# Four GpSimd operations tied behind VectorE's activation operation, and the engine orders solved anew

## The chip, the cores and the metric

The kernel runs on one core of a Trainium2 chip. A core has five engines with a queue each: TensorE (PE: matmuls; PEld: its weight loads), VectorE (DVE), ScalarE (ACT), GpSimd (POOL) and SyncE (SP, which here only issues DMAs). Each engine takes its instructions in order, and instructions of different engines meet only at semaphores. The metric is the device time of one execution in microseconds; before the change it is 293.84 us, the median of 3 runs (292.66 to 293.95).

## The reference

Two layers follow each other, in float32, for 8 batches of 576 tokens and 8 heads of 64:

```python
q_s = softmax(q, axis=-1)                 # over the 64 of a head
k_s = softmax(k, axis=2)                  # over the 576 tokens
kv  = einsum('bhsd,bhde->...', k_s, v)    # 64x64 per batch and head
x   = (q_s @ kv) as [4608 tokens, 512]
h   = x @ w_in                            # 512 -> 2048
g   = where(h > 0, h, exp(min(h, 0)) - 1) # ELU
out = g @ w_out                           # 2048 -> 512
```

## The kernel before

**Units of attention.** Each batch is two units n (16 in all, two per batch). For a unit the kernel loads q, k and v (576 KB each), takes `exp` of q and k on ScalarE (lines 392, 396, 416), row sums of q and their reciprocals on VectorE (418, 420), multiplies q by them (430, mostly GpSimd; tile QS), copies v to bfloat16 (a cast at line 274; tile VB), transposes QS (by TensorE for units 0 to 3, line 454; by a DMA transpose `turn`, line 467, from unit 4, whose result is copied into qsT by `widen`, again line 274), multiplies k by v on TensorE (`kv_mm`, 504), scales that into MBLK (513, 517) and multiplies MBLK by qsT (`ao_mm`, 535; `ao_parts`, 547). The result is copied from PSUM into XT (`xt`, line 274). Units 2 and 3 use one qsT buffer in turn.

**Blocks of the second layer.** The 4608 tokens are nine blocks j of 512. For each there are eight hidden groups g of 256 rows: `hg_mm` (line 617, eight matmuls of 128x512) writes a pair of PSUM banks, and `hg` makes the ELU of it. There are two forms of that. Form "a": ScalarE takes `exp` (643) and `relu(1-e)` (645), and VectorE ends it with `scalar_tensor_tensor` on two halves (649). Form "d", used for every second group of blocks 0 and 1 alone: ScalarE takes `exp` (643), VectorE takes min and add in place on the SBUF tile ESB (`tensor_scalar`, 654: this is the "activation operation" of the change), then a `tensor_tensor` max against PSUM (656). A block's next `hg_mm` on the same bank pair waits for the end of that. Two pairs of banks alternate, and ESB has two buffers. Blocks 0 and 1 multiply by `w_out` plainly (`out_mm`, 670). From block 2 on a product with seven in place of eight partial multiplications is used (`pair`, `mms`, 803): it needs combinations of the weights (`combos`, 730; tiles TB and W) and of the activations (`add_sum`, 754; tiles SB and GR), and its partial results are added at line 812.

**What sets the order.** The program adds 1395 operations, numbered as they are added, each with what it reads and writes; from that come its dependencies. `ORDER` lists, for each engine, the numbers in the order in which the engine takes them. An operation that may run on two engines goes to the one whose list holds its number. `Sched.order` merges the five lists into one program with modelled durations; `emit` turns each dependency on another engine into a semaphore wait. The lists are fixed text: nothing is decided on the chip. Spare matmuls (line 889) fill TensorE's first microseconds.

The operations that the change and the prediction name, all in the profile's stretch from 15 to 110 us:

| number | what it is | engine before | engine after |
|---|---|---|---|
| 68, 69, 70, 73 | loads: q of unit 2, `w_out` parts 0 and 1, q of unit 3 (GpSimd's queue) | POOL | POOL, order 69, 68, 70, 73 |
| 77, 76 | loads of v and k of unit 3 | POOL, 77 first | POOL, 76 first |
| 114, 122, 124, 137, 140 | exp of q of unit 2; ELU of block 0, group 6 (exp, max); exp and row sum of q of unit 3 | ACT, DVE | the same engines |
| 138 | exp of k of unit 3 | ACT | ACT |
| 151 | `ao_mm` of unit 2, second part | PE | PE, one `out_mm` earlier |
| 154 | copy of unit 3's transposes into qsT (after 151 has read it) | DVE | ACT |
| 146, 152 | `xt` copies of unit 2 | DVE | ACT |
| 179, 185, 188 (and 182) | copies of block 0's output from PSUM | DVE (182 ACT) | ACT |
| 166, 173 | `xt` copies of unit 3 | ACT | ACT, behind the eight above |
| 192, 194 | `hg_mm` of block 1, group 1, first and second half | PE | PE |
| 249, 250, 195 | exp and relu of block 1, group 1; exp of group 0 | ACT | ACT |
| 196, 255, 268, 281 | `tensor_scalar` (654) of block 1, groups 0, 2, 4, 6 | DVE | DVE |
| 197, 256, 269, 282 | `tensor_tensor` max (656) of the same | DVE | DVE |
| 253, 266, 279 | `hg_mm` of block 1, groups 2, 4, 6 | PE | PE |
| 208, 234, 237 | casts of v of units 5, 6, 7 | POOL | POOL |
| 210 | `widen` of unit 4 | POOL | ACT |
| 227, 300 | QS of units 5 and 6 | POOL | POOL |
| 239 | `kv_mm` of units 6 and 7 | PE | PE |
| 390 | a weight combination of group 1 | POOL, after 237 | POOL, ahead of 237 |
| 305, 316 | `xt` copies of units 6 and 7, first parts | ACT | DVE |
| 369 | copy of a block-1 output | ACT | DVE |
| 419 | row sum of q of unit 9 | DVE | DVE, ahead of block 3's 405 and 406 |

Of the kernel before, what the change touches and what calls it, by code (L numbers as in the profile page):

```python
# [11 lines left out]
B, H, S, D = 8, 8, 576, 64  # L12
# [12 lines left out]
ISSUE = {"sp": 550, "act": 550, "gp": 740}  # L25
ORDER = {
# [23 lines left out]
    "act": (  # L50
# [11 lines left out]
    "dve": (  # L62
# [37 lines left out]
}  # L100


class Op:
    __slots__ = ("eng", "dur", "emit", "deps", "key", "idx", "start", "end",
                 "dma", "sem", "val", "clock", "nbytes", "side", "early", "alts")

    def __init__(self, eng, dur, emit, key, dma=None, nbytes=0):
        self.eng, self.dur, self.emit, self.key = eng, dur, emit, key
# [938 lines left out]
        for i in range(4):  # L1047
            one[i]()
            two[i]()


S_ = S
# [32 lines left out]
```

## Time and profile before

| | |
|---|---|
| median of 3 runs | 293.84 us (292.66 to 293.95) |
| the profiled execution | 294.51 us, of which 292.7 us are the span from first to last instruction |
| busy: PE, DVE, ACT, POOL | 280.9, 234.7, 207.3, 165.7 us |
| mean granted TensorE clock | 0.999 |

The page gives busy times, the span in 40 slices and the chain of work that ended last. A busy PE counts pipelined matmuls with modelled ends, so a stall of TensorE is read best from the starts of its matmuls. In a row of the timeline come the start, the duration, the engine, the line, the operation and its tiles, the number of instructions merged, and in brackets the idle time before it and what ended that.

### The profile page before, as it was taken

Reading aid. Unit: us, or ns where it says so; the run is one execution under the profiler, and the core shown is the slowest. Engines: PE = TensorE matmul, PEld = TensorE weight load, DVE = VectorE, ACT = ScalarE, POOL = GpSimd, SP = SyncE. Lnnn points to the kernel's source line nnn. Section 1 sums busy time; section 2 is a strip of 40 time slices with the busy share of each in tenths; the row PEclk is TensorE's granted clock in tenths of the full one; section 3 lists DMA queues with packets and bytes.
Section 4 is the critical chain, followed back from the end, with each engine's and each line's share of the span. In section 5 each row is a group of like instructions: output and inputs, shape, how many; then the busy total and the mean of one; then the engine's idle time right before and its main releaser. Section 6 shows DMA issues by size and latency. Waiting matters only on the chain.

```text
span 292.7 us, 5471 instructions
## 1 busy us (share of the span) xinstructions
PE 280.9 (96%) x2176; PEld 243.2 (83%) x2176; DVE 234.7 (80%) x434; ACT 207.3 (71%) x227; POOL 165.7 (57%) x162
## 2 busy tenths in 40 slices
PE   2899999989999999999999999999999999999995
PEld 0478787767888889998999899899999999989994
DVE  3648848898878989969998989689888767698793
ACT  4868716958979988976987869967765636665520
POOL 2892445642756569577538383669505571575930
PEclk9999999999999999999999999999999999999999
DMA  7999997879996485937762926451302003200315
GB/s 264 399 365 389 388 389 261 246 230 287 273 215 250 140 216 136 274 82 236 145 198 57 279 59 186 142 107 38 76 18 56 0 17 74 54 0 20 92 38 143
DMA packets 36475, 50.04 MB, mean 171 GB/s; under 512 B 16353, under 2 KB 18145, under 8 KB 36449
## 3 DMA queue, kind: packets, MB, share of 16 engines
q1 hardware_dynamic: 29680, 33.96, 41.9%
q0 software_dynamic: 6528, 15.47, 17.5%
q8 instruction: 17, 0.28, 0.4%
q10 hardware_dynamic: 240, 0.26, 0.3%
q14 instruction: 10, 0.07, 0.1%
HBM read 36.70 MB, written 9.44 MB: 158 GB/s over the span
## 4 chain that ended last, share of the span: by engine, by line
PE 83%; DMA 7%; DVE 3%; POOL 3%; ACT 1%; issue 0%; SPq 0%
PE PS L617 38%; PE PS L803 32%; PE PS L670 9%; DMA W<-in_moe_w_out_dram 5%; PE PS L535 2%; DMA KR<-in_k_dram 2%; POOL W L374 2%; PE PS L504 2%; DVE ESB L654 1%; DVE GR L656 1%; ACT ESB L643 1%; DVE GR L649 0%; POOL VB L274 0%; PE PS L454 0%; POOL QS L430 0%
## 5 line engine op out<-in xcount | busy, mean ns | idle before, releaser
L617 PE MATMUL PS<-XT,W 128*128 128x512 f32 x576 | 142.3, 393 | 1.4 <-DVE GR L656 1.4
L617 PEld LDWEIGHTS PS<-XT,W 128*128 128x128 f32 x576 | 104.9, 188 | 23.1 <-DVE GR L656 2.2
L649 DVE SCALAR_TENSOR_TENSOR GR<-PS,GE 128x512 fp32r<-128x512 f32 x112 | 76.7, 687 | 19.9 <-ACT GE L645 18.5
L643 ACT ACTIVATE GE<-PS 128x1024 f32<-128x1024 f32 x56 | 57.4, 1024 | 40.6 <-PE PS L617 33.0
L754 POOL TENSOR_TENSOR GR<-GR 128x256 fp32r<-128x256 f32 (+1 forms) x55 | 50.9, 946 | 28.4 <-PE PS L803 22.8
L645 ACT ACTIVATE GE<-GE 128x1024 f32<-128x1024 f32 x56 | 59.4, 1061 | 1.5
L803 PE MATMUL PS<-W,GR 128*128 128x256 f32 x336 | 53.7, 283 | 0.0
L803 PE MATMUL PS<-TB,GR 128*128 128x256 f32 x336 | 52.2, 283 | 0.0
L803 PEld LDWEIGHTS PS<-W,GR 128*128 128x128 f32 x336 | 47.1, 191 | 1.2
L803 PEld LDWEIGHTS PS<-TB,GR 128*128 128x128 f32 x336 | 46.5, 191 | 1.1
L430 POOL TENSOR_TENSOR QS<-QR,RZQ 128x1152 f16<-128x1152 f32 (+1 forms) x16 | 31.1, 1941 | 24.0 <-DVE RZQ L420 22.8
L812 DVE TENSOR_TENSOR OSB<-OSB,PS 128x256 f32<-128x256 f32 x84 | 34.4, 416 | 8.1 <-PE PS L803 6.8
L670 PE MATMUL PS<-W,GR 128*128 128x512 f32 x128 | 33.1, 397 | 0.2 <-DMA W<-in_moe_w_out_dram 0.2
L754 POOL TENSOR_TENSOR SB<-GR 128x256 fp32r<-128x256 f32 (+1 forms) x19 | 17.2, 909 | 25.7 <-DVE GR L649 15.3
L754 POOL TENSOR_TENSOR GR<-SB,GR 128x256 fp32r<-128x256 f32 (+1 forms) x18 | 18.5, 1034 | 16.9 <-PE PS L803 16.7
L670 PEld LDWEIGHTS PS<-W,GR 128*128 128x128 f32 x128 | 23.2, 188 | 5.3 <-DMA W<-in_moe_w_out_dram 0.7
L418 DVE TENSOR_REDUCE ZQ<-QR 128x18 f32<-128x1152 f32 (+2 forms) x18 | 21.7, 1208 | 6.4 <-ACT QR L416 5.1
L396 ACT ACTIVATE KR<-KR 128x1152 bf16<-128x1152 f32 x16 | 18.3, 1155 | 8.4 <-DMA KR<-in_k_dram 8.4
L643 ACT ACTIVATE ESB<-PS 128x1024 f32<-128x1024 f32 x16 | 16.1, 1024 | 6.9 <-PE PS L617 5.9
L754 DVE TENSOR_TENSOR GR<-GR 128x256 fp32r<-128x256 f32 (+1 forms) x29 | 19.5, 675 | 0.3
L274 POOL CAST VB<-VR 128x1152 bf16<-128x1152 f32 (+1 forms) x11 | 11.9, 1083 | 12.9 <-DMA VR<-in_v_dram 10.8
L803 PE MATMUL PS<-W,SB 128*128 128x256 f32 x104 | 17.6, 282 | 0.0
(62 smaller groups left out, 272.1 us busy)
## 6 DMA issues: line engine op xcount, KB each, us to landing
out_dram<-OSB SPq DMA_DIRECT2D x61, 128.0 KB, 2.5
QR<-in_q_dram SPq DMA_DIRECT2D x12, 576.0 KB, 4.6
KR<-in_k_dram SPq DMA_DIRECT2D x12, 576.0 KB, 4.8
VR<-in_v_dram SPq DMA_DIRECT2D x12, 576.0 KB, 5.4
W<-in_moe_w_out_dram POOLq DMA_DIRECT2D x4, 1024.0 KB, 17.0
QR<-in_q_dram POOLq DMA_DIRECT2D x4, 576.0 KB, 11.8
VR<-in_v_dram POOLq DMA_DIRECT2D x4, 576.0 KB, 13.3
KR<-in_k_dram POOLq DMA_DIRECT2D x4, 576.0 KB, 11.1
```

What stands on the lines that cost most here:

```text
L274: return e.activation(dst, src, AF.Copy) if e is self.nc.scalar else e.tensor_copy(dst, src)
L396: S.add("act", t_act(1152, False), lambda e: e.activation(ek[:, :, :, :].rearrange("p h c d -> p (h c d)"), flat(k), AF.Exp), key - 2, X=[ ...
L418: S.add("dve", t_dve(m), lambda e, qp=qp, zp=zp: e.tensor_reduce(zp, qp, AX.X, ALU.add), key - 3, R=[f"qR{i}{x}" for x in xs], W=[f"ZQ{i}{ ...
L430: lambda e, qp=q[:, :, a:b, :], rz=rz, dst=qs[:, :, a:b, :]: e.tensor_tensor(dst, qp, rz, ALU.mult),
L617: last = e.matmul(P[:, t * 512:(t + 1) * 512], self.W1[:, kc, tt * 128:(tt + 1) * 128], self.XT[:, kc, rc:rc + BLK], start=(kc == 0), stop ...
L643: S.add("act", t_act(1024, True), lambda e: e.activation(ge, P, AF.Exp), key, W=own, X=banks)
L645: S.add("act", t_act(1024, False), lambda e: e.activation(ge, ge, AF.Relu, bias=1.0, scale=-1.0), key, X=own)
L649: S.add("dve", t_dve(512 if j else 1024), lambda e, u=u: e.scalar_tensor_tensor(*(x[:, :, u, :] if j else x for x in (gt, P)), 0.0, ge[:, ...
L670: last = e.matmul(dst, self.tile(jb, jj, ts), self.W2[:, jj, c0:c1], start=(jj == 0), stop=(jj == 15))
L754: lambda e: e.tensor_tensor(dst, a, b, op), key, R=R, W=W, X=X, after=after)
L803: last = e.matmul(dst, a[i][:, y_, :], b[i][:, y_, :], start=start and i == 0 and y_ == 0, stop=stop and i == len(grps) - 1 and y_ == z - ...
L812: S.add("dve", t_dve(256), lambda e: e.tensor_tensor(dst, a, b, ALU.add), key, R=R, W=W, X=X, after=after)
```

## The change

Four dependencies are added at the end of the program, so that four GpSimd operations wait for VectorE's line 654 in block 1: the cast of v of unit 5 for group 0, QS of unit 5 for group 2, the cast of v of unit 6 for group 4, QS of unit 6 for group 6. All five lists of `ORDER` are replaced from about the seventieth operation on. 125 operations change their engine: 40 go from GpSimd to VectorE and 37 back, 24 from VectorE to ScalarE and 12 back, 7 from ScalarE to GpSimd and 5 back. No operation is added or removed, and TensorE's operations stay the same in number and size.

```diff
     "act": (
-        "3 29 25 41 22 36 23 45 53 34 38 39 58 66 67 90 93 94 96 100 101 104 111 112 114 122 134 "
-        "109 135 137 126 115 138 182 198 173 166 224 249 250 195 199 207 254 260 261 267 297 273 "
-        "274 221 280 230 236 286 287 233 293 294 308 334 240 335 343 344 407 352 353 305 317 358 "
+        "3 29 25 41 22 36 23 45 53 34 38 39 58 66 90 93 94 96 100 101 104 111 112 114 108 122 134 "
+        "109 137 135 126 115 146 154 152 138 179 182 198 185 188 173 166 224 249 250 195 207 199 "
+        "254 260 261 210 267 297 273 274 221 280 223 230 286 232 287 233 293 294 236 334 335 308 "
...
     "dve": (
-        "106 113 117 123 118 108 124 119 140 141 142 136 128 129 130 146 152 179 154 160 161 162 "
-        "185 174 167 201 188 202 225 251 252 196 197 255 256 212 262 213 226 214 263 215 216 217 "
-        "268 269 298 275 276 223 281 299 282 232 288 289 386 348 295 296 309 339 241 310 242 336 "
+        "105 106 113 117 123 118 124 119 140 141 136 142 128 129 130 160 161 162 174 167 201 202 "
+        "225 226 251 252 196 197 255 256 262 263 212 213 214 215 216 217 268 269 275 276 281 298 "
+        "282 299 288 289 348 295 296 240 241 242 243 336 337 244 245 309 246 310 345 305 346 354 "
...
     "gp": (
-        "1 32 14 15 24 16 17 18 48 40 19 20 21 68 69 70 73 72 71 74 75 77 76 120 131 116 143 163 "
-        "144 139 164 132 200 205 203 208 210 227 234 300 237 390 394 318 303 311 387 410 314 395 "
+        "1 32 14 15 24 16 17 18 48 40 19 20 21 69 68 70 73 72 71 74 75 76 77 120 131 116 143 163 "
+        "144 139 132 164 200 205 203 208 227 234 300 390 237 394 303 386 318 311 399 388 410 392 "
...
     "sp": (
-        "8 9 10 11 12 13 204 206 209 219 228 187 184 218 180 235 229 189 302 238 301 190 349 350 "
+        "8 9 10 11 12 13 204 206 183 180 187 189 186 209 228 190 218 219 235 229 301 302 184 238 "
...
+AFTER = ((208, 196), (227, 255), (234, 268), (300, 281))
...
             one[i]()
             two[i]()
+        for a, b in AFTER:
+            S.ops[a].deps.setdefault(S.ops[b], "raw")
```

In SP's list 204 and 228 are DMA transposes, 206, 209, 218, 219, 229 and 235 loads of units 6 and 7, and 180 to 190 the eight output stores of block 0 (128 KB each): five of the stores now stand ahead of 209, the load of v of unit 6.

119 rows, old and new, of the table ORDER are left out of this document.

## The prediction

> **What bounds the kernel now.** I read the page first (busy times, clock, the chain that ended last), then busy times by stretch, then what TensorE waited for, and then the timeline of the one stretch in which it waited.
>
> ```profile
> span 292.7 us, 5471 instructions
> PE 280.9 (96%) x2176; PEld 243.2 (83%) x2176; DVE 234.7 (80%) x434; ACT 207.3 (71%) x227; POOL 165.7 (57%) x162
> ...
> PEclk9999999999999999999999999999999999999999
> ...
> PE 83%; DMA 7%; DVE 3%; POOL 3%; ACT 1%; issue 0%; SPq 0%
> ```
>
> TensorE is busy for 96% of the span at full clock, and is 83% of the chain. The change leaves its work alone, so the time can move only by what TensorE waits. The next rows give, for three stretches, the busy time of PE, PEld, DVE, ACT and POOL in turn:
>
> ```profile
> 14.00:50.00 36.00, 35.78 (x274) 28.57 (x275) 25.14 (x38) 22.26 (x26) 18.58 (x23) 1.00 1.22 357
> 50.00:72.00 22.00, 20.55 (x158) 15.89 (x157) 19.53 (x29) 16.89 (x18) 10.45 (x8) 1.00 0.86 257
> 72.00:289.00 217.00, 217.00 (x1680) 195.56 (x1678) 182.53 (x349) 158.80 (x172) 129.55 (x119) 1.00 0.45 121
> ```
>
> From 72 to 289 us TensorE is never idle; from 14 to 50 it loses 0.2 us; the loss is in 50 to 72, which is block 1, where VectorE has 19.53 of 22 us. What TensorE waited for there, and line 654 over the whole run (minimum, median, maximum in ns):
>
> ```profile
> PE PS L617 <- DVE GR L656: 1.4, 2, 0.9
> ```
> ```profile
> L654 DVE TENSOR_SCALAR ESB<-ESB x8: 683/690/1612, 19.5 to 69.6; 128x1024 f32<-128x1024 f32 x8
> ```
>
> Two waits for line 656; and line 654 just ahead of it takes 0.69 us as a rule and 1.61 at worst. The timeline shows where:
>
> ```profile
> 56.11 1.15 POOL L274 CAST VB<-VR 128x1152 bf16<-128x1152 f32 x1 [2.23 <-DMA VR<-in_v_dram]
> 56.23 1.94 ACT L643 ACTIVATE ESB<-PS 128x1024 f32<-128x1024 f32 x2 [0.32 <-DVE GR L656]
> ...
> 57.20 1.15 POOL L274 CAST qsT<-QT 128x1152 fp32r<-128x1152 f16 x1
> 57.29 1.61 DVE L654 TENSOR_SCALAR ESB<-ESB 128x1024 f32<-128x1024 f32 x1 [1.09 <-ACT ESB L643]
> ...
> 58.54 0.73 PE L670 MATMUL PS<-W,GR 128*128 128x512 f32 x2
> ...
> 58.93 1.22 DVE L656 TENSOR_TENSOR GR<-ESB,PS 128x1024 fp32r<-128x1024 f32 x1
> ...
> 60.21 2.11 PE L617 MATMUL PS<-XT,W 128*128 128x512 f32 x8 [0.94 <-DVE GR L656]
> ...
> 63.33 1.15 POOL L274 CAST VB<-VR 128x1152 bf16<-128x1152 f32 x1
> 63.42 1.61 DVE L654 TENSOR_SCALAR ESB<-ESB 128x1024 f32<-128x1024 f32 x1 [0.46 <-ACT ESB L643]
> ...
> 65.07 1.22 DVE L656 TENSOR_TENSOR GR<-ESB,PS 128x1024 fp32r<-128x1024 f32 x1
> 65.35 0.51 PE L535 MATMUL PS<-qsT,MBLK 128*128 128x384 f32 x2
> ...
> 66.34 2.11 PE L617 MATMUL PS<-XT,W 128*128 128x512 f32 x8 [0.48 <-DVE GR L656]
> ```
>
> Both long ones start while a GpSimd cast is running (57.20 to 58.35, 63.33 to 64.48) and end 0.55 us after it: VectorE got nothing done until the cast had ended. Each costs 1.61 - 0.69 = 0.92 us, and 656 and then `hg_mm` of group 4 (60.21) and group 6 (66.34) come that much later. What TensorE loses is read from starts. Eight matmuls of 128x512 take 1.82 to 1.84 us (rows further down), 0.23 each; from 58.54 to 60.21 two are done, so 1.67 - 0.46 = 1.2 us are lost; at 65.35 two narrower ones take some 0.35, so 0.99 - 0.35 = 0.64.
>
> **The change part by part.**
>
> *The four waits.* 208 is the cast at 56.11: it waited for the load of its v, when 196 was long over, so its wait adds nothing. 227 and 300 already stood behind 255 and 281, since both need VectorE's later reciprocal: nothing. 234 is the cast at 63.33; it now starts after 268, which falls to 0.69, and is 0.8 us later. Behind it on GpSimd stand 300 and what follows; who waits for its VB is 239 at 77 us, so more than 10 us of TensorE's work hide it. The other collision (cast at 57.20) is 210, and no wait touches it: the new lists move it to ScalarE. Gain at group 4: 255 is worth 0.92 and TensorE loses 1.2 there, so 0.92. Gain at group 6: 0.64, all that is lost there. Sum -1.56.
>
> *ScalarE ahead of block 1.* ScalarE takes six copies that VectorE had (146, 154, 152, 179, 185, 188), all listed ahead of 173 and 166, which `hg_mm` 194 waits for:
>
> ```profile
> 35.84 1.14 ACT L274 ACTIVATE qsT<-PS 128x1152 fp32r<-128x1152 f16 x1 [0.92 <-PE PS L454]
> ...
> 43.59 0.40 PE L535 MATMUL PS<-qsT,MBLK 128*128 128x256 f32 x2
> ...
> 45.15 1.16 ACT L396 ACTIVATE KR<-KR 128x1152 bf16<-128x1152 f32 x1 [7.12 <-DMA KR<-in_k_dram]
> 46.22 0.58 ACT L274 ACTIVATE OSBX<-PS 128x512 f32<-128x512 f32 x1
> ...
> 46.69 1.16 ACT L392 ACTIVATE QR<-QR 128x1152 f32<-128x1152 f32 x1
> ...
> 48.63 0.72 ACT L274 ACTIVATE XT<-PS 128x256 fp32r<-128x256 f32 x2 [0.78 <-PE PS L535]
> 49.25 1.16 ACT L392 ACTIVATE QR<-QR 128x1152 f32<-128x1152 f32 x1
> ```
> ```profile
> 50.77 1.03 ACT L643 ACTIVATE ESB<-PS 128x1024 f32<-128x1024 f32 x1 [0.36 <-PE PS L617]
> ```
>
> 154 overwrites the qsT that 151 reads. 151 (43.59) moves ahead of one `out_mm` of four matmuls (0.91) and ends at some 43.1. Then ScalarE, in its new order: 154 to 44.3 (1.14), 152 to 44.9 (0.6, as 46.22), 138 to 46.0 (its load goes ahead of v's 576 KB now, so it need not wait until 45.15), 179 and 182 to 47.2, 198 to 48.4, 185 and 188 to 49.5, 173 and 166 (0.39 and 0.44) to 50.4. Before they ended at 49.35. TensorE would start 194 at 49.6 and gets it at 50.5: a new stall of 0.9 us. Bounds: 0, if ScalarE's copies run earlier than I have them, and 1.1, the whole delay of 166. I take 0.9. Block 1's chain (250, then 251, 252, 196, 197, 254, 255, 256) hangs on 194, so 256 ends at about 60.15, where it ended before: 0.92 won and 0.9 lost.
>
> *Loads on GpSimd's queue.* With `w_out` part 0 ahead of it, q of unit 2 comes 1024 KB later, 2.9 us at the 357 GB/s of the first stretch. 114 waits for it, and 122 and 124 stand behind 114.
>
> ```profile
> 34.95 1.35 DVE L418 TENSOR_REDUCE ZQ<-QR 128x18 f32<-128x1152 f32 x1 [1.24 <-ACT QR L392]
> ```
>
> Cover: this is 140, before which VectorE idled 1.24 us. Without it the cost is up to 2.9 - 1.24 = 1.7 us; but q need not have come just in time before, and TensorE waits in this stretch for `w_out` part 1, whose place is unchanged. I take 0. The five stores ahead of 209 hold SP for some 3 us and v of unit 6 with it; its cast is 234, and the same 10 us up to 239 hide it.
>
> *GpSimd at 72 us.* 390 goes ahead of the cast 237, which 239 needs:
>
> ```profile
> 70.57 2.13 POOL L430 TENSOR_TENSOR QS<-QR,RZQ 128x1152 f16<-128x1152 f32 x1 [6.08 <-DVE RZQ L420]
> 73.40 1.15 POOL L274 CAST VB<-VR 128x1152 bf16<-128x1152 f32 x1 [0.70 <-DMA VR<-in_v_dram]
> 75.16 3.56 POOL L730 TENSOR_TENSOR TB<-W 128x512 fp32r<-128x512 f32 x2 [0.61 <-DVE GR L649]
> 77.87 0.78 PE L504 MATMUL PS<-VB,KR 64*64 64x65 bf16 x72
> ```
>
> 390 waits for the last ELU of block 1 (VectorE, some 74.5), takes 1.3 to 2.2 (the pair takes 3.56), the cast 1.15: ready at 77.0 to 77.9. TensorE, with the work ahead of 239 in the new order, wants it at 77.6. Cost 0 to 0.4; I take 0.2.
>
> *The weight combinations, 86 to 107 us.*
>
> ```profile
> 86.00:107.00 21.00, 21.00 (x179) 18.02 (x178) 17.96 (x28) 19.32 (x22) 12.36 (x9) 1.00 0.68 202
> ```
> ```profile
> 87.12 2.41 POOL L730 TENSOR_TENSOR W<-W 128x1024 fp32r<-128x1024 f32 x1 [3.34 <-PE PS L670]
> 88.75 1.34 DVE L754 TENSOR_TENSOR SB<-GR 128x512 fp32r<-128x512 f32 x1
> ...
> 94.06 0.68 DVE L754 TENSOR_TENSOR GR<-GR 128x512 fp32r<-128x512 f32 x1
> ```
>
> VectorE gains 316, 369, 387, 395, 401, 419, 444 and 457 there (some 6.0 us) and loses 307, 388, 392, 393, 397, 399 and 459 (5.0): 17.96 becomes 19.0 of 21. An addition that meets a GpSimd instruction takes 1.34 for 0.68 (88.75 ends 0.56 after the GpSimd instruction). 406 frees the bank for block 3's third group; by the list it ends 0 to 0.6 us after TensorE wants it. I take 0.3.
>
> *The rest, to 289 us.* VectorE gets lighter: it gives 24 copies to ScalarE and takes 12, some 12 x 0.6 = 7 us over the run, and its additions nearly balance (40 come, 37 go). TensorE is never idle there, so there is little to win:
>
> ```profile
> 73.17 1.84 PE PS L617 x8
> ...
> 75.92 1.82 PE PS L617 x8
> ```
>
> 0.02 us for each of some 55 such groups, 1.1 us at most. What can be lost is open: a stall like the one at 58.54 costs 1.2. I take 0.
>
> The sum: -1.56 + 0.9 + 0.2 + 0.3 = -0.2 us. Against the profiled execution 294.51 becomes 294.3; that execution is 0.67 above the median, so the median goes from 293.84 to 293.6.
>
> **The rivals.**
>
> *The waits pay in full.* ScalarE is early enough for 194 and nothing else is late: -1.56, or 292.3, and to 291.2 with the 1.1 us of the rest. For it: ScalarE sat idle for 7.12 us before 45.15, and VectorE has less work. Against it: 154 can use that idle time only after 151.
>
> *The collision moves to the additions.* Before, three additions between 86 and 107 us were held up. In the new list ten combinations and additions of VectorE stand there, while GpSimd's list is as full as before but without gaps, as 388, 392, 393, 397 and 399 come over. If half pay the 0.66 us of row 88.75, that is 3.3 on 19.0, 22.3 of 21 us: 1.3 us of stall at block 3's third group. It decides from 2 us of such waits on. The lists of blocks 3 to 8 are remade too (some 70 additions change sides); one more stall of that size gives +2.6 and, with the sum above, 296.2. For it: VectorE has 182.53 of 217 us. Against it: before, the same traffic cost nothing after 72 us.
> The Trainium skill ("SBUF — State Buffer", section "SBUF: two separate sides") states the reason: VectorE and GpSimd share a pair of ports under an exclusive lock held for a whole instruction, and VectorE needs it in its two-port mode or with two SBUF inputs. The first half is what 57.29 shows and the four waits cure; the second half, which 88.75 bears out, speaks against the change, as no wait guards the additions. By that rule alone the sum would be this rival's, 296.2; by the rows, which show the same traffic without a stall of TensorE, it is 293.6.
>
> *The change does nothing.* 255 and 268 stay at 1.61 because another GpSimd instruction comes in their place: then only the new costs are left, +1.4, 295.2. Little speaks for it: 227 is tied behind 255, and 234 behind 268.
>
> **How the numbers follow.** Half a per cent (1.5 us) is about what can be told from no change. Little net change, with the third rival in it: 0.42, predicted 293.6, its own range 292.4 to 295.2. In full: 0.20. Collision moved, or a stall of that kind elsewhere: 0.38. The range of 291.8 to 296.8 reaches into both. Faster 0.20, same 0.42, slower 0.38.
>
> **What would show it.** Right: line 654 at no more than 0.70 in block 1; a wait of line 617 for 656 of at most 0.3 at group 4 and none at group 6; a new idle of TensorE near 50 us that ends with ScalarE's XT copy. Wrong: no stall near 50 us (then 292.3), or TensorE waits between 100 and 289 us for 649, 754 or 812.

## The result and the profile after

The changed kernel takes 292.54 us (median of 13 executions, 292.20 to 293.24), the kernel before, beside it on the same chip, 294.38 us (13 executions, 292.66 to 295.01). The ratio is 0.9945, with a 95% interval of 0.9931 to 0.996: 0.55% faster, some 1.6 us (the two medians are 1.84 apart). The forecast was 293.6 us in a range of 291.8 to 296.8, with "no change" as the likeliest case. The number lies in the range, but only because the range was wide enough to hold a rival as well: what happened is the case that had 0.20, the first rival, in which the removed collisions are paid out in full (292.3 us).

The profiled execution of after took 293.22 us, 1.29 less than the profiled one of before. It is one of three of the thirteen above 293.1 us; the other ten lie between 292.20 and 292.74. Its page, first the span, then busy times, then the chain that ended last by engine:

```profile
span 291.4 us, 5465 instructions
...
PE 280.8 (96%) x2176; PEld 243.6 (84%) x2176; DVE 225.4 (77%) x425; ACT 209.8 (72%) x237; POOL 168.1 (58%) x161
...
PE 88%; DMA 7%; POOL 3%; SPq 0%; issue 0%; DVE 0%
```

TensorE's work is the same to 0.1 us, VectorE is busy for 9.3 us less, and VectorE's share of the chain went from 3% to 0. The three stretches again (stretch, its length, then busy time of PE, PEld, DVE, ACT, POOL, granted clock, DMA share, GB/s):

```profile
14.00:50.00 36.00, 35.57 (x274) 28.39 (x273) 21.63 (x33) 25.19 (x33) 17.85 (x24) 1.00 1.25 369
50.00:72.00 22.00, 21.97 (x165) 17.39 (x165) 17.31 (x26) 19.54 (x21) 8.67 (x7) 1.00 0.96 249
72.00:289.00 217.00, 215.75 (x1674) 194.43 (x1672) 179.73 (x348) 155.99 (x173) 134.64 (x119) 1.00 0.46 122
```

Block 1 (50 to 72) now has TensorE busy for 21.97 of 22 us, where it was 20.55. The 215.75 in the last stretch is no loss: TensorE's last group of matmuls starts at 285.68 us in place of 287.03, so its work ends 1.3 us before the stretch does. What TensorE waited for in the changed kernel, all that the profile lists, and line 657 (it was 654) over the run:

```profile
PE PS L892 <- ACT QR L419: 5.3, 1, 5.3
PE PS L550 <- DVE MBLK L520: 0.6, 1, 0.6
PE PS L507 <- ACT VB L277: 0.5, 1, 0.5
PE PS L673 <- DMA W<-in_moe_w_out_dram: 0.3, 1, 0.3
PE PS L507 <- POOL VB L277: 0.2, 1, 0.2
```
```profile
L657 DVE TENSOR_SCALAR ESB<-ESB x8: 683/689/695, 19.7 to 68.2; 128x1024 f32<-128x1024 f32 x8
```

The two waits of `hg_mm` for the ELU (1.4 us) are gone, no other wait of `hg_mm` (now line 620) took their place, and the longest `tensor_scalar` is 0.695 us instead of 1.612. The timeline shows groups 2, 4 and 6 of block 1:

```profile
56.64 1.15 POOL L277 CAST VB<-VR 128x1152 bf16<-128x1152 f32 x1 [2.51 <-DVE GR L659]
...
57.66 0.69 DVE L657 TENSOR_SCALAR ESB<-ESB 128x1024 f32<-128x1024 f32 x1 [1.09 <-ACT ESB L646]
...
58.51 2.12 POOL L433 TENSOR_TENSOR QS<-QR,RZQ 128x1152 f16<-128x1152 f32 x1 [0.71 <-DMA QT<-QS]
...
59.54 1.15 ACT L277 ACTIVATE qsT<-QT 128x1152 fp32r<-128x1152 f16 x1
...
59.66 3.94 PE L620 MATMUL PS<-XT,W 128*128 128x512 f32 x16
...
62.87 0.69 DVE L657 TENSOR_SCALAR ESB<-ESB 128x1024 f32<-128x1024 f32 x1 [0.21 <-ACT ESB L646]
...
65.15 1.98 PE L620 MATMUL PS<-XT,W 128*128 128x512 f32 x8
```

The cast of unit 4 (210, the row at 59.54) is on ScalarE, and GpSimd's next instruction (227) starts after 255 has ended. The row at 56.64 (208) names VectorE's line 659 as what ended the wait, but 208 does not depend on that line: the load of its v landed at 56.52, 0.12 us ahead of its start, and line 659 happened to end at 56.56. Group 4's `hg_mm` starts at 59.66 in place of 60.21, group 6's at 65.15 in place of 66.34.

To follow the gain along the run I compare the starts of TensorE's matmuls in two traces at the same amount of TensorE work done, after minus before, worked out from all matmul rows:

| place in before's time | after minus before, us |
|---|---|
| 15 us, ahead of any moved work | +0.24 |
| 39 us | +0.27 |
| 52 us, `hg_mm` 194 is done | +0.36 |
| 58 us, ahead of group 4 | +0.39 |
| 63 us, behind group 4 | -0.56 |
| 67 us, within group 6 | -1.24 |
| 70 us, behind group 6 | -1.33 |
| 115 us | -1.34 |
| 288 us | -1.36 |

The first +0.27 belongs to the execution and not to the change: at 39 us the same lists with one wait and with none (below) have about -0.2 and -0.5, and before's lists with other edits -0.4 to -0.6. Behind it, two steps make the whole gain: -0.95 at group 4 and -0.77 at group 6.

### The profile page after: what moved, and what is told of

Read it like the earlier page. It is cut to its first block, busy times and chain, and to the rows that moved or that the text cites. A ratio compares the mean times of both kernels' runs of the same rounds, so it can differ in the third digit from the quotient of the medians.

```text
span 291.4 us, 5465 instructions
## 1 busy us (share of the span) xinstructions
PE 280.8 (96%) x2176; PEld 243.6 (84%) x2176; DVE 225.4 (77%) x425; ACT 209.8 (72%) x237; POOL 168.1 (58%) x161
## 4 chain that ended last, share of the span: by engine, by line
PE 88%; DMA 7%; POOL 3%; SPq 0%; issue 0%; DVE 0%
PE PS L620 41%; PE PS L806 32%; PE PS L673 10%; DMA W<-in_moe_w_out_dram 5%; PE PS L538 3%; DMA KR<-in_k_dram 2%; POOL W L377 2%; PE PS L507 2%; POOL VB L277 0%; PE PS L457 0%; POOL QS L433 0%; SPq L359 0%; POOL W L385 0%; POOL QR L359 0%; DVE OSB L815 0%
## 5 line engine op out<-in xcount | busy, mean ns | idle before, releaser
L757 POOL TENSOR_TENSOR GR<-GR 128x256 fp32r<-128x256 f32 (+1 forms) x48 | 47.3, 999 | 31.4 <-DVE SB L757 16.5
L806 PE MATMUL PS<-TB,GR 128*128 128x256 f32 x336 | 51.3, 283 | 0.0
L806 PEld LDWEIGHTS PS<-TB,GR 128*128 128x128 f32 x336 | 45.7, 191 | 0.7
L433 POOL TENSOR_TENSOR QS<-QR,RZQ 128x1152 f16<-128x1152 f32 (+1 forms) x16 | 30.5, 1905 | 20.6 <-DVE RZQ L423 19.8
L757 POOL TENSOR_TENSOR GR<-SB,GR 128x256 fp32r<-128x256 f32 (+1 forms) x18 | 17.4, 975 | 24.5 <-PE PS L806 12.7
L757 POOL TENSOR_TENSOR SB<-GR 128x256 fp32r<-128x256 f32 (+1 forms) x20 | 19.3, 968 | 13.7 <-DVE GR L652 6.3
L757 DVE TENSOR_TENSOR GR<-GR 128x256 fp32r<-128x256 f32 (+1 forms) x36 | 21.3, 603 | 0.6 <-PE PS L806 0.6
L277 ACT ACTIVATE XT<-PS 128x512 fp32r<-128x512 f32 (+6 forms) x23 | 13.6, 595 | 6.2 <-PE PS L538 3.2
```

The costliest lines, as they stand in the source:

```text
L277: return e.activation(dst, src, AF.Copy) if e is self.nc.scalar else e.tensor_copy(dst, src)
L433: lambda e, qp=q[:, :, a:b, :], rz=rz, dst=qs[:, :, a:b, :]: e.tensor_tensor(dst, qp, rz, ALU.mult),
L757: lambda e: e.tensor_tensor(dst, a, b, op), key, R=R, W=W, X=X, after=after)
L806: last = e.matmul(dst, a[i][:, y_, :], b[i][:, y_, :], start=start and i == 0 and y_ == 0, stop=stop and i == len(grps) - 1 and y_ == z - ...
```

## The experiments

The theory with which they were made: the whole gain comes from two collisions of GpSimd's casts with line 654; moving 210 to ScalarE takes one away, the waits take away the other or keep others from coming, and the re-solved lists do nothing else. The rivals: the remade lists win (or lose) time elsewhere; the waits do nothing; ScalarE's lead ahead of 194 is luck or not needed. All kernels of this section compute the whole result. "The kernel before" is always timed beside them on the same chip.

**The four waits alone.**

```diff
 (the kernel before, its lists unchanged)
+        for a, b in ((208, 196), (227, 255), (234, 268), (300, 281)):
+            S.ops[a].deps.setdefault(S.ops[b], "raw")
```

> The four waits on the old orders, nothing else. Theory A (the whole gain is two collisions of line 654 with GpSimd casts, 0.9 us of TensorE at group 4 and 0.7 to 0.8 at group 6): only the cast of v of unit 6 is held back, so 268 falls from 1.61 to 0.69 us, 255 stays at 1.61 behind 210, the wait at group 6 goes and the one at group 4 stays: -0.64 to -0.8 us, ratio 0.997 to 0.998. Theory B (the re-solved orders carry the gain, the waits do nothing): ratio 1.000, line 654 unchanged.

Measured: 293.13 us (12 executions), ratio 0.9984 (0.9972 to 0.9996), where 0.997 to 0.998 was expected. By this ratio the waits alone are worth 0.16% of the 0.55%; by the medians (293.13 against 293.95) it is 0.28%, half of it. The profiled execution was the fastest of the twelve, 292.28 us, and its timeline shows something that I had not thought of:

```profile
56.73 0.69 DVE L654 TENSOR_SCALAR ESB<-ESB 128x1024 f32<-128x1024 f32 x1 [1.09 <-ACT ESB L643]
56.74 1.69 POOL L274 CAST qsT<-QT 128x1152 fp32r<-128x1152 f16 x1
```

The cast 210, which no wait guards, is still on GpSimd. Here 255 started ahead of it, by 0.015 us in the records, and took its usual 0.69 us, and the cast took 1.69 in place of 1.15. So the cast lost 0.54 us, where in the kernel before VectorE was second and lost 0.92. In this execution TensorE made the whole gain, some 1.65 us on before between 39 and 70 us. Nine of the twelve executions lie within 292.95 to 293.54, about 0.85 us above the profiled one, which fits one collision lost; no profile of such an execution was taken, so that is argued from the times.

**210 on ScalarE alone.**

```diff
 "act": ... 254 260 261
+210
 267 297 ...
 "gp":  ... 203 208
-210
 227 234 ...
```

> The old orders without the waits, with operation 210 alone taken from GpSimd to ScalarE, behind 261. Theory A: 255 falls to 0.69, 268 keeps its collision with the cast of v of unit 6; group 4 comes 0.9 us earlier: -0.9 us, ratio 0.997; or the collision at 268 goes too, if the whole stretch shifts 0.9 us ahead of the cast, whose load does not shift: then -1.6. Theory B: ratio 1.000 within 0.1%, since ScalarE gets more work and VectorE none less.

Measured: 293.15 us (12 executions, 291.96 to 294.41), ratio 0.997 (0.9957 to 0.9983). In the profiled execution (293.26 us) neither 255 nor 268 was slowed: 234 started 0.2 us after 268 and lost (1.48 us). Between 39 and 70 us TensorE won 1.74 us on before, and between 90 and 115 us it gave 1.04 back. The timeline there:

```profile
82.97 1.15 POOL L274 CAST qsT<-QT 128x1152 fp32r<-128x1152 f16 x1 [1.31 <-DMA QT<-QS]
...
86.16 2.42 POOL L730 TENSOR_TENSOR W<-W 128x1024 fp32r<-128x1024 f32 x1
...
86.51 2.62 DVE L754 TENSOR_TENSOR SB<-GR 128x512 fp32r<-128x512 f32 x1
...
99.65 2.12 PE L617 MATMUL PS<-XT,W 128*128 128x512 f32 x8 [0.44 <-DVE GR L649]
```

The addition 398 (86.51) stood behind GpSimd's combination 387 until 88.58 and took 2.62 us, where before has 1.34; VectorE was late from there on and TensorE waited for its ELU at 99.65. This is the second rival's mechanism (the collision moves to the additions), at its place, in a kernel that the forecast was not about.

**The same program in another execution.**

> The same program as with the cast 210 on ScalarE and no waits, looked at once more, since its times lay near 293.15 us while the profiled execution had neither 255 nor 268 slowed and lost its gain later instead. Theory one: the usual loss is in the second block; then 268 meets GpSimd's 234 again and line 654 has a largest duration of 1.4 us or more. Theory two: the usual loss is among the combinations at 86 to 101 us; then both 255 and 268 are at 0.69 us, and the addition 398 takes 1.3 us or more (2.62 in the first look, 0.68 where nothing holds it).

Measured: 292.45 us, one execution. The same view, and line 654:

```profile
85.08 2.41 POOL L730 TENSOR_TENSOR W<-W 128x1024 fp32r<-128x1024 f32 x1 [0.73 <-PE PS L670]
...
86.70 1.34 DVE L754 TENSOR_TENSOR SB<-GR 128x512 fp32r<-128x512 f32 x1
```
```profile
L654 DVE TENSOR_SCALAR ESB<-ESB x8: 683/689/697, 19.6 to 67.5; 128x1024 f32<-128x1024 f32 x8
```

Both conditions of theory two hold, yet nothing was lost: 398 took 1.34 us and TensorE had no wait for it. What differs is 387, which began 1.08 us earlier, since the cast of QT ahead of it on GpSimd (82.97 above) had not waited for its DMA transpose. So 1.34 us costs nothing here and 2.62 costs 1.0. Which of the two is the usual one in this program stays open: of its 13 executions three are below 292.5 us and ten at 292.9 or more, and only two were profiled.

**Both by hand, without the re-solved lists.** The two edits above together, all else as before.

> The old orders with 210 on ScalarE and the four waits: two small edits, without the re-solved lists. Theory A: both collisions gone, all four of block 1's line 654 at 0.69, -1.6 us, ratio 0.9945, the same as the changed kernel. Theory B: at most half of the changed kernel's gain, ratio 0.997 or more.

Measured: 292.22 us (5 executions, 292.11 to 292.42), ratio 0.9945 (0.9933 to 0.9957), the ratio of the changed kernel. Line 654:

```profile
L654 DVE TENSOR_SCALAR ESB<-ESB x8: 683/690/712, 19.1 to 67.4; 128x1024 f32<-128x1024 f32 x8
```

One moved cast and four waits give the whole gain (with 210 moved alone it was 0.997, 0.9957 to 0.9983); the other 124 changes of engine and the new orders give, in sum, nothing that can be measured. In the old lists the wait that binds is that of 234 for 268. With 210 moved alone, 268 started only 0.22 and 0.14 us ahead of 234 in the two profiled executions. Here the load for 234 landed at 62.06, 0.10 us after 268 had started, and 234 began at 62.73, when 268 had ended. That 268 loses to 234 in other executions without the waits is argued from the times and in no trace.

**The re-solved lists without the waits.**

```diff
-AFTER = ((208, 196), (227, 255), (234, 268), (300, 281))
+AFTER = ()
```

> The changed kernel without its four waits. In the changed kernel 208, 234 and 300 waited for a load or a reciprocal, not for line 654; only 227 is held back by its wait, to 0.16 us after 255 ended. Without it 227 can start when 208 ends, at 57.8, with 255 starting at 57.7. Theory A, waits needed: 227 takes the place of the cast, 255 is held up to 2 us and group 4 comes 1.4 to 2.0 us later: ratio 0.999 to 1.001. Theory B, the orders suffice: 255 starts first, ratio 0.9945 as for the changed kernel.

Measured: 292.71 us (7 executions, 292.27 to 293.71), ratio 0.9964 (0.9951 to 0.9977). By the two ratios the waits are worth some 0.2% in the new lists, but the intervals overlap (0.9951 to 0.9977, and 0.9931 to 0.996 with the waits), so this is a hint and not a measurement; neither of the two theories (0.999 to 1.001, or 0.9945) was met. The profiled execution (292.71 us) shows how near it is without them:

```profile
56.82 0.69 DVE L657 TENSOR_SCALAR ESB<-ESB 128x1024 f32<-128x1024 f32 x1 [1.09 <-ACT ESB L646]
...
57.27 2.22 POOL L433 TENSOR_TENSOR QS<-QR,RZQ 128x1152 f16<-128x1152 f32 x1 [0.77 <-DMA QT<-QS]
```

QS of unit 5 (227) overwrites the tile QS that the DMA transpose of unit 4 reads. It starts when that transpose has landed, 0.45 us after 255: the DMA decides which comes first. Here 255 was first and lost nothing.

**One wait alone.**

```diff
-AFTER = ((208, 196), (227, 255), (234, 268), (300, 281))
+AFTER = ((227, 255),)
```

> The changed kernel with one of its four waits, 227 behind 255. Theory A says that on the new orders this is the only wait that binds (208, 234 and 300 come late by their loads and reciprocals anyway): all line 654 of block 1 at 0.69, ratio 0.9945, and no execution near 293.2 because of group 4. If another wait binds in some executions, the median lies between 0.9945 and the 0.9964 of the orders alone.

Measured: 292.48 us (6 executions, 292.31 to 292.74), ratio 0.9947 (0.9932 to 0.9962). The kernel with this one wait is as fast as the one with all four. GpSimd's row shows that the wait binds:

```profile
57.93 2.12 POOL L433 TENSOR_TENSOR QS<-QR,RZQ 128x1152 f16<-128x1152 f32 x1 [1.68 <-DVE ESB L657]
```

The transpose of unit 4 had landed at 57.30, and 227 stood until 255 (57.15 to 57.85) had ended. But 255 had started 0.14 us ahead of the landing, so it would have been first here without the wait too.

**XT late by one wait.** The last but one of ScalarE's `xt` copies for 194 (173, with 166 behind it) is made to start behind VectorE's copy 167, to test whether block 1 hangs on these copies at all.

```diff
-AFTER = ((208, 196), (227, 255), (234, 268), (300, 281))
+AFTER = ((208, 196), (227, 255), (234, 268), (300, 281), (173, 167))
```

> The changed kernel with one more wait: ScalarE's XT copy 173 waits for VectorE's XT copy 167, which ended at 49.71 while 173 started at 49.08. So 166 ends some 0.65 us later. The prediction's walk held that TensorE's 194 hangs on 166 and block 1's chain on 194: then 194 starts 0.5 to 0.6 us later and all that follows stays that much later, ratio to the kernel before 0.9964 to 0.997. If ScalarE has slack there, no change: 0.9945.

Measured: 293.09 us (12 executions), ratio 0.9978 (0.9964 to 0.9992), where 0.9964 to 0.997 was expected; the median is 0.6 us above that of the version with one wait beside it.

```profile
48.98 0.71 ACT L277 ACTIVATE XT<-PS 128x256 fp32r<-128x256 f32 x2 [0.56 <-DVE XT L277]
...
49.74 6.97 PE L620 MATMUL PS<-XT,W 128*128 128x512 f32 x28 [0.44 <-ACT XT L277]
```

TensorE loses 0.7 us at 194 (its place against before goes from -0.50 at 39 us to +0.20 at 52) and does not get it back: the two steps behind it are as large as in the changed kernel, -0.9 and -0.8. So what the forecast's second step says holds: whatever ScalarE is late by at 194 is paid in full. Only, in the changed kernel ScalarE is not late.

**A collision put back.** The cast 208 is made to wait for TensorE's 258, so that it is running when 255 starts.

```diff
-AFTER = ((208, 196), (227, 255), (234, 268), (300, 281))
+AFTER = ((208, 258), (227, 255), (234, 268), (300, 281))
```

> The changed kernel with one wait exchanged: the cast 208 waits for TensorE's 258 (ended at 57.35) in place of 196, so that it runs from about 57.4 to 58.6 and 255 (57.66) starts inside it. If the collision is the cause by itself: 255 takes 1.4 to 1.6 us, 266 comes 0.7 to 0.9 us later and the time rises by 0.7 to 0.9 us, ratio to the kernel before 0.997 to 0.9975. If what mattered was VectorE's load or the orders: 255 at 0.69 and ratio 0.9945.

Measured: 293.35 us (12 executions), ratio 0.9979 (0.9968 to 0.999).

```profile
56.83 1.15 POOL L277 CAST VB<-VR 128x1152 bf16<-128x1152 f32 x1 [3.10 <-PE PS L673]
57.05 1.47 DVE L657 TENSOR_SCALAR ESB<-ESB 128x1024 f32<-128x1024 f32 x1 [1.09 <-ACT ESB L646]
...
58.03 0.91 PE L507 MATMUL PS<-VB,KR 64*64 64x65 bf16 x72 [0.34 <-POOL VB L277]
...
59.83 0.50 PE L620 MATMUL PS<-XT,W 128*128 128x512 f32 x1 [0.23 <-DVE GR L659]
```

The cast was first by 0.22 us, 255 took 1.47 and ended 0.54 us behind it. The price, 0.87 us against the version with one wait beside it, is not the collision's alone. The places of TensorE against before are -0.60 at 39 us, -0.22 at 52, +0.20 at 58 and -0.40 at 63. So some 0.4 us is lost in this execution by 52 us, ahead of what the edit touches, some 0.4 to the late cast, which also holds `kv_mm` (58.03, 0.34 us), and the step at group 4 is 0.60 in place of the 0.9 of the kernels without the collision: 0.3 us, part of the collision being hidden behind the wait of `kv_mm`. The sign is shown; a price of 0.9 us for this collision alone is not.

**The kernel before once more.**

> The kernel before, once more, for a second profile. If the two collisions are its usual state: line 654 of groups 2 and 4 at 1.61 again, waits of line 617 for 656 at both groups, near 294 us.

Measured: 294.56 us.

```profile
L654 DVE TENSOR_SCALAR ESB<-ESB x8: 682/689/1607, 19.5 to 69.6; 128x1024 f32<-128x1024 f32 x8
```

255 took 1.512 and 268 1.607 us: both collisions stand in both profiled executions of before.

## Why the prediction was right and wrong

The forecast had named a sign of being wrong: no stall near 50 us (then 292.3). That is what came.

**What bounds the kernel, and what the collisions are worth: right.** Gain at group 4: predicted 0.92, measured 0.95. Group 6: predicted 0.64, measured 0.77; there I had counted only what TensorE lost in one row. The port rule cited from the Trainium skill ("SBUF — State Buffer", section "SBUF: two separate sides") agrees in both directions with these runs: 255 at 1.47 us behind a cast that was 0.22 us ahead, a cast at 1.69 behind a 255 that was 0.015 us ahead in the records.

**The step that failed: "ScalarE ahead of block 1 ... a new stall of 0.9 us".** Its mechanism is right, as the late XT shows; its size is wrong, 0.9 for a measured 0.1 (the place of TensorE goes from +0.27 at 39 us to +0.36 at 52, and no wait of line 620 is left). The ScalarE rows of the changed kernel, in the order that the step foresaw:

```profile
42.95 0.40 PE L538 MATMUL PS<-qsT,MBLK 128*128 128x256 f32 x2
...
43.39 1.13 ACT L277 ACTIVATE qsT<-PS 128x1152 fp32r<-128x1152 f16 x1 [1.38 <-PE PS L538]
44.42 0.59 ACT L277 ACTIVATE XT<-PS 128x512 fp32r<-128x512 f32 x1
44.89 1.17 ACT L399 ACTIVATE KR<-KR 128x1152 bf16<-128x1152 f32 x1
...
45.95 1.09 ACT L277 ACTIVATE OSBX<-PS 128x512 f32<-128x512 f32 x2
...
46.90 1.19 ACT L395 ACTIVATE QR<-QR 128x1152 f32<-128x1152 f32 x1
...
47.96 1.23 ACT L277 ACTIVATE OSBX<-PS 128x512 f32<-128x512 f32 x2
...
49.08 0.71 ACT L277 ACTIVATE XT<-PS 128x256 fp32r<-128x256 f32 x2
```

The chain starts at 43.39, where I had 43.16 (44.3 - 1.14); that difference is the shift of this execution, +0.27 at 39 us. It ends at 49.79 (49.08 + 0.71), 6.40 us later, where I had 50.4, 7.24 us later. The ten instructions one by one have recorded durations of 1.13, 0.59, 1.17, 0.60, 0.61, 1.19, 0.62, 0.60, 0.38 and 0.44, in sum 7.33 (7.325 to the nanosecond), 0.92 us more than the chain took. I had added durations, and an instruction of ScalarE starts before the recorded end of the one ahead of it (43.39 + 1.13 = 44.52, the next starts at 44.42): by 0.10 to 0.13 us at eight of the nine places, not at all at the ninth. So the chain is 7.24 - 6.40 = 0.84 us shorter than I had it, and the term falls from 0.9 to about 0.1. A row of this kind was in the forecast already: 46.22 + 0.58 = 46.80, and the next ACT row starts at 46.69. The Trainium skill ("ScalarE: Activation LUTs", section "What ACT_TABLE_LOAD costs") states an overlap of about 93 ns between activations that follow each other; the trace agrees in kind, with 103 to 131 ns at those eight places. With starts in place of durations the term is 0.1 and the sum -1.56 + 0.1 = -1.5 before the two small terms.

**"GpSimd at 72 us ... I take 0.2": 0.** The combination 390 and the cast 237 in the changed kernel:

```profile
73.90 1.29 POOL L733 TENSOR_TENSOR TB<-W 128x512 fp32r<-128x512 f32 x1 [0.21 <-DVE GR L652]
...
75.14 1.14 POOL L277 CAST VB<-VR 128x1152 bf16<-128x1152 f32 x1
...
77.44 0.78 PE L507 MATMUL PS<-VB,KR 64*64 64x65 bf16 x72
```

390 took 1.29, the low end that I gave, and the cast ended at 76.28, 1.2 us before `kv_mm` started. The high end of 2.2 came from before's 390, which had been held up itself: a combination on VectorE started at 75.00, 0.16 us ahead of it.

**"The weight combinations ... I take 0.3": 0.** TensorE is busy for all of 86 to 107 us, and VectorE's busy time there was foreseen as 19.0 us and is 19.53; what matters is who was first, in the timeline below the stretch:

```profile
86.00:107.00 21.00, 21.00 (x180) 18.03 (x179) 19.53 (x31) 19.16 (x22) 15.19 (x11) 1.00 0.72 195
```

```profile
87.44 0.68 DVE L757 TENSOR_TENSOR SB<-GR 128x512 fp32r<-128x512 f32 x1
88.04 1.22 DVE L733 TENSOR_TENSOR W<-W 128x1024 fp32r<-128x1024 f32 x1
```
```profile
88.20 2.21 POOL L757 TENSOR_TENSOR GR<-GR 128x512 fp32r<-128x512 f32 x1 [2.57 <-DVE SB L757]
```

The combination 387, now on VectorE, started 0.16 us before GpSimd's addition 399, and the loser was GpSimd, which took 2.21 us in place of some 1.3 (its other additions of this size, in the median), ended at 90.41 and held TensorE up nowhere. The second rival had VectorE as the loser of each meeting ("if half pay the 0.66 us"); here the loser was the one that came second. That rival has its place in the version with 210 moved alone (2.62 us at 86.51), not here, so its 0.38 was too much for the changed kernel, and the first rival's 0.20 too little: most of the 0.42 hung on the 0.9 of ScalarE.

**The four waits: right in sum, wrong in one reason.** "227 and 300 already stood behind 255 and 281, since both need VectorE's later reciprocal" is true of the old lists. In the new ones 226 (that reciprocal) stands ahead of 255 in VectorE's list, and 227 is free to start as soon as the transpose of unit 4 has landed. There the wait can hold, as it did in the version with one wait (57.93 above, released by line 657). In the profiled execution of the changed kernel itself it held nothing: 255 had ended at 58.35 when the transpose landed at 58.38. And in all five profiled executions of the new lists 255 started before that landing, by 0.12 to 0.72 us, so that the wait spares 255 a collision in other executions is argued from their times alone. 208 started 1.3 us after 196 had ended (54.62 + 0.68 = 55.30, and 56.64), so that its wait held nothing, and 239 did not wait for 234's cast, as foreseen.

**Loads: right.** q of unit 2 came about 1.5 us later (its `exp` starts at 29.78 us, 28.23 before, and waits 1.25 us for the load; 0.24 of it is the general shift), and the row that I named as cover, the row sum of unit 3, starts at 35.19 for 34.95, the general shift. **The rest to 289 us: right**, -1.34 at 115 us and -1.36 at 288.

**Left open.** What an execution of "waits alone" at 293.1 us looks like inside, whether and where the waits save time in the new lists (no profiled execution of them has a slow `tensor_scalar`, other than where the collision was put back), and how often 398 meets 387 in the version with 210 moved alone.

## What to carry to other kernels

Add up a chain on one engine from starts to starts in the trace, not from durations: ten ScalarE instructions were 0.92 us shorter than their sum, which was nearly the whole gap between "no change" and "faster". When VectorE and GpSimd meet, ask which of the two starts first and who waits for the loser; a semaphore wait on the engine that has slack fixes the order. In the old lists four waits, of which the trace shows one to bind (234 behind 268), and one moved cast gave the whole gain, so try such a version by hand before solving all lists anew. A wait that holds nothing in the old order (227 behind 255) can hold in the new one: look at the changed lists for what now stands ahead.

## What was unexpected of the hardware

A shift of 0.1 us turns the outcome round. In the kernel before, 255 started 0.09 us behind the cast 210 (57.29 and 57.20) and took 1.61 us; in the kernel with the waits alone it started 0.015 us ahead of it (56.725 and 56.740) and took 0.69, and the cast paid 0.54 us instead. A lead that small cannot be taken from the records at its word: in the same trace the cast 210 starts 0.06 us before the recorded end of the cast ahead of it on GpSimd.

So one program can have executions near 1 us apart. The version with 210 moved alone was profiled once at 293.26 and once at 292.45 us, with 398 at 2.62 and 1.34 us; the difference goes back to a cast that waited 1.31 us for its DMA transpose in the one and not in the other. The kernel with the waits alone ranges from 292.28 to 294.85; that this has the same kind of cause is not shown.
